# Mamba-2 scan and SiLU block on one core: unit 0's second y bank copied by VectorE, and the first 385 entries in a new order

## The chip, the core and the metric

The kernel runs on one NeuronCore of a Trainium2 chip. Five engines with a queue each work side by side: TensorE (PE, with its weight loads as PEld), VectorE (DVE), ScalarE (ACT), GpSimd (POOL) and SyncE (SP), which here only issues DMAs. Instructions of one engine run in the order in which they were written; a semaphore wait at the head of a queue holds everything behind it. Matmuls write PSUM, which is read by VectorE and ScalarE. The metric is the device time of the whole program in microseconds (us). The kernel before has a median of 329.49 us over 3 runs (328.6 to 329.88).

## What is computed

A chunked state-space scan over 4 batches, 8 heads and 768 positions (head size 32, state size 16), then a feed-forward block with SiLU over the 3072 resulting rows of 256:

```python
log_a = np.log(np.clip(a, 1e-06, 1.0))
for c in range(nc):                       # chunks of the sequence
    cum = np.cumsum(la, axis=-1)
    L = np.exp(cum[:, :, :, None] - cum[:, :, None, :]) * causal
    M = np.einsum('bhin,bhjn->bhij', Cc, Bc) * L
    y_intra = np.einsum('bhij,bhjd->bhid', M, xc)
    y_inter = np.einsum('bhin,bhnd->bhid', Cc, state) * np.exp(cum)[:, :, :, None]
    y[:, :, sl] = y_intra + y_inter
    state = decay_full[:, :, None, None] * state + np.sum(Bx, axis=2)
# then, with x = y as 3072 rows of 256
h = x @ w_in                              # 256 x 2048
out = (h * (1.0 / (1.0 + np.exp(-h)))) @ w_out    # 2048 x 256
```

The two weight matrices come in as 8-byte numbers, so each tile of them is turned into 4-byte numbers on the chip.

## The kernel before

The 3072 positions are 12 units of 256 (three to a batch); two units make a pair, so there are six pairs. Each unit passes through the scan (a few small matmuls, and elementwise work on VectorE, ScalarE and GpSimd) and gives y; each pair then passes through w_in, SiLU and w_out. Pair 0 takes the feed-forward block in plain 4-byte matmuls (`f_s1`, `f_n`); the later pairs take it in split operands of a faster matmul type.

Nothing schedules the kernel when it is built. The text `SCHEDULE` lists 1309 entries; each is a short name with numbers, and the last loop of the kernel calls the function of each entry in turn (`DO`). So the place of an entry in the text is the place of its instructions in the queue of their engine, and of its DMA in the queue that issues it (`QUEUES`: 0 is SP, 1 is ACT, 2 is POOL). `SLOTS` says which buffer of a pool each new tile takes, by an explicit list: `s2k` and `r4k` are SBUF slots, `raw` the slots for incoming weights, `hp` three PSUM banks that rotate under most matmul results.

The entries that matter here, for unit u (lines of the kernel before in brackets):

- Loads. `Lt,u,1,g` is a quarter of C in the layout that VectorE transposes, four of them for a unit (L262); `Ln` is half of B or C (L254), `Lx` half of x (L269), `ia` and `ip` parts of a (L375, L379), `lw,n` one weight tile of 512 KB: 0 to 7 of w_in, 8 to 15 of w_out (L288). All of these are on SP, except two `Ln` of unit 0 on ACT.
- `z` is one matmul of zeros that keeps TensorE busy and whose result is not used (L441); there are 36 of them, all in the opening.
- Decays. `A` clips a (L448); `AT` transposes it on TensorE (L453) and `AU` copies it out (L457); `as` spreads it (L495 on VectorE, L497 on ScalarE); `ab` transposes that (L502); `E` is a scan on VectorE that makes the decay matrix of one half unit (L512). `P01` makes the running products (L475, L479).
- Scan of unit 0 and 1. `T` transposes C on VectorE and needs all four `Lt` (L525); `ce` scales it on ScalarE (L546); `tp` and `tq` transpose B and copy it out (L531, L540); `B` and `C` are products on GpSimd or VectorE (L520, L551); `D` is the state matmul, which needs both halves of x and of `B` (L571); `g0` is C times B (L585); `M` multiplies it by the decays on VectorE, two halves (L600); `S` advances the state, four steps (L613, L615); `SM` masks it on ScalarE, two halves (L623); `Y` is the matmul that gives y in two PSUM banks, `ga` and `gb` (L635, L644).
- `X0,u,w` copies one y bank out of PSUM on ScalarE (L666); the two copies of a unit fill its part of the tile that `s` reads.
- Pair 0 in w_in. `s,u,j` is the matmul of unit u with weight tile j (L697; four matmuls, 128x256 each, two records each in the trace); `si` is its SiLU on ScalarE (L703). `n1` is a matmul with a tile of w_out (L761). `a`, `d` and `q` are the matmuls of later pairs (L800, L782).
- Weights. `u` and `v` take the two words of a weight tile apart on ScalarE (L294, L297); `w,n,0`, `w,n,1`, `w,n,2` work on them on VectorE (L303, L307, L310); `W` adds them on GpSimd (L318). `H`, `lD`, `dD`, `Wl`, `Wd` make the split operands (L322 to L335).

Of the kernel before, what the change touches and what calls it, by code (L numbers as in the profile page):

```python
# [888 lines left out]
```

## Time and profile before

| | us |
|---|---|
| median of 3 runs | 329.49 |
| profiled execution, whole time | 329.1 |
| its span, first to last instruction | 327.4 |
| TensorE busy | 320.3 |
| VectorE busy | 240.4 |
| ScalarE busy | 209.5 |
| GpSimd busy | 56.0 |

The span is 1.7 us shorter than the execution's own time. Times in the rows of the trace count from the start of the span. In a timeline row the first number is the start, the second how long the row lasts, then the engine (with a q where it is the queue that issues a DMA), the line, the operation, what it writes and reads, the shapes, and how many instructions are merged; in square brackets stands how long the engine was idle just before and what ended that. In a row of windows stand the stretch, its length, then for each engine the busy time and the number of instructions, the granted clock, the share of the DMA engines in use and GB/s.

### The profile page before, as it was taken

To read this page: it belongs to the slowest core of one execution; us is meant where nothing else is said; L and a number is where in the kernel's file an instruction comes from. 1 tells how busy PE (TensorE), PEld (TensorE's weight loads), DVE (VectorE), ACT (ScalarE), POOL (GpSimd) and SP (SyncE) were. 2 spreads that over 40 slices of the span, in tenths; PEclk is the share of its full clock that TensorE was granted. 3 is DMA by queue.
4 is the path that set the end of the run, shared out by engine and by line. 5 is a ranking of instruction groups with operands and counts; after the bars stand their busy time and mean duration, and the time that the engine had idled before them with its cause. 6 is when DMAs were issued, how large, how long until landed. Compare 5 with 4: busy or idle time off the path is not lost.

```text
span 327.4 us, 7519 instructions
## 1 busy us (share of the span) xinstructions
PE 320.3 (98%) x3064; PEld 243.4 (74%) x3067; DVE 240.4 (73%) x331; ACT 209.5 (64%) x319; POOL 56.0 (17%) x74
## 2 busy tenths in 40 slices
PE   8999999999999999999999999999999999999994
PEld 3478576655687777878887778878887788888883
...
DMA packets 94962, 29.27 MB, mean 89 GB/s; under 512 B 80000, under 2 KB 86912, under 8 KB 94928
## 3 DMA queue, kind: packets, MB, share of 16 engines
...
q14 instruction: 10, 0.08, 0.1%
...
## 4 chain that ended last, share of the span: by engine, by line
PE 94%; SPq 2%; DMA 1%; DVE 1%; issue 1%; DVEq 0%
PE hp L782 29%; PE ga L800 18%; PE gb L800 18%; PE hp L761 9%; PE hp L697 6%; PE o_ps L782 6%; PE ga L635 2%; PE ga L585 2%; PE ga L644 2%; DMA s2k<-in_C_dram 1%; PE gb L644 1%; PE ga L571 1%; SPq L262 0%; SPq L375 0%; PE o_ps L531 0%
## 5 line engine op out<-in xcount | busy, mean ns | idle before, releaser
L782 PE MATMUL hp<-r4k,s2k 128*128 128x512 f32 x400 | 110.0, 394 | 0.0
L651 DVE SCALAR_TENSOR_TENSOR r4k<-r4k,r4k 128x1024 fp32r<-128x1024 f32 (+1 forms) x42 | 50.5, 1202 | 51.3 <-ACT r4k L827 48.2
L782 PEld LDWEIGHTS hp<-r4k,s2k 128*128 128x128 f32 x400 | 74.0, 188 | 16.4 <-issue 0.3
L800 PE MATMUL ga<-raw,s2k 128*128 128x512 f32 x240 | 62.3, 395 | 0.0
L800 PE MATMUL gb<-raw,s2k 128*128 128x512 f32 x240 | 61.1, 390 | 0.0
L800 PEld LDWEIGHTS ga<-raw,s2k 128*128 128x128 f32 x240 | 44.7, 188 | 11.4 <-ACT ga L811 0.9
L800 PEld LDWEIGHTS gb<-raw,s2k 128*128 128x128 f32 x240 | 44.8, 188 | 9.9 <-ACT gb L811 0.5
L837 DVE SCALAR_TENSOR_TENSOR r4k<-r4k,r4k 128x1024 fp32r<-128x1024 f32 x40 | 49.2, 1231 | 3.4 <-DVE r4k L651 0.9
L827 ACT ACTIVATE r4k<-r4k 128x1024 fp32r<-128x1024 f32 x40 | 42.2, 1058 | 3.2 <-issue 1.3
L811 ACT ACTIVATE ga<-ga 128x1024 f32<-128x1024 f32 x21 | 21.1, 1007 | 24.6 <-PE ga L800 23.8
L811 ACT ACTIVATE gb<-gb 128x1024 f32<-128x1024 f32 x21 | 21.2, 1009 | 17.6 <-PE gb L800 13.3
L782 PE MATMUL o_ps<-r4k,s2k 128*128 128x512 f32 x80 | 30.7, 390 | 0.0
L761 PE MATMUL hp<-r4k,s2k 128*128 128x512 f32 x64 | 30.0, 602 | 0.0
L821 ACT ACTIVATE r4k<-gb 128x1024 f32<-128x1024 f32 x21 | 21.4, 1021 | 12.4 <-PE gb L800 9.9
L520 POOL TENSOR_TENSOR BT<-bn,ab 128x256 f32<-128x256 f32 x10 | 6.7, 672 | 129.5 <-DVE ab L512 123.3
L318 POOL TENSOR_TENSOR s2k<-s2k,s2k 128x512 uint32<-128x512 uint32 (+1 forms) x19 | 23.6, 1250 | 26.4 <-DVE s2k L307 13.7
L821 ACT ACTIVATE r4k<-ga 128x1024 f32<-128x1024 f32 x21 | 21.5, 1023 | 8.4 <-PE ga L800 8.2
L512 DVE TENSOR_TENSOR_SCAN ab<-ab,diag 128x512 f32<-128x512 f32 x20 | 24.8, 1265 | 0.0
L697 PE MATMUL hp<-r4k,s2k 128*128 128x256 f32 x96 | 22.3, 382 | 0.2 <-issue 0.2
L697 PEld LDWEIGHTS hp<-r4k,s2k 128*128 128x128 f32 x96 | 18.0, 190 | 4.0 <-issue 1.4
L761 PEld LDWEIGHTS hp<-r4k,s2k 128*128 128x128 f32 x64 | 11.6, 189 | 10.5 <-issue 9.6
L782 PEld LDWEIGHTS o_ps<-r4k,s2k 128*128 128x128 f32 x80 | 15.0, 188 | 3.2
...
## 6 DMA issues: line engine op xcount, KB each, us to landing
...
raw<-in_moe_w_in_dram SPq DMA_DIRECT2D x8, 512.0 KB, 4.2
raw<-in_moe_w_out_dram SPq DMA_DIRECT2D x8, 512.0 KB, 8.0
...
```

Of the source, the lines that this page charges most:

```text
L318: nc.gpsimd.tensor_tensor(out=u[:, :, fs], in0=u[:, :, fs], in1=v[:, :, fs], op=ALU.add)
L512: nc.vector.tensor_tensor_scan(out=o, data0=src, data1=diag.rearrange("p h t -> p (h t)"), initial=0.0, op0=ALU.mult, op1=ALU.add)
L644: nc.tensor.matmul(out=y[w][32 * q:32 * q + 32, c, 64 * k:64 * k + 64], lhsT=xc[64 * c:64 * c + 64, k, h], rhs=m[64 * c:64 * c + 64, k, h] ...
L651: nc.vector.scalar_tensor_tensor(out=l, in0=f32(h), scalar=BACK, in1=y, op0=ALU.mult, op1=ALU.add)
L697: nc.tensor.matmul(out=hp[:, i], lhsT=WT[j][:, kc, 128 * i:128 * i + 128], rhs=XM()[:, 2 * kc:2 * kc + 2, u], start=(kc == 0), stop=(kc == ...
L761: nc.tensor.matmul(out=NP[m], lhsT=WT[8 + f // 2][:, f % 2, 128 * m:128 * m + 128], rhs=GT[0, f // 2][:, f % 2], start=(n == 1), stop=(n = ...
L782: nc.tensor.matmul(out=ACC[P, c], lhsT=WK[8 + i, p][:, k, 128 * m:128 * m + 128], rhs={"h": HT, "l": LT, "d": DT}[p][P, i][:, k], start=(n ...
L800: nc.tensor.matmul(out=o, lhsT=WK[j, q][:, kc, 128 * i:128 * i + 128], rhs=xs[:, 2 * kc:2 * kc + 2], start=(start and q == "h" and kc == 0 ...
L811: nc.scalar.activation(t, t, AF.Copy, scale=1.0 + Z)
L821: nc.scalar.activation(g, t, AF.Silu, scale=BACK)
L827: nc.scalar.activation(t, GT[G, i], AF.Copy, scale=-LESS * Z)
L837: nc.vector.scalar_tensor_tensor(out=DT[G, i], in0=f32(HT[G, i]), scalar=-1.0, in1=f32(LT[G, i]), op0=ALU.mult, op1=ALU.subtract)
```

## The change

One function is new, and one entry uses it: unit 0's bank 1 of y, before the entry `X0,0,1` on ScalarE, is now copied by `Xd,0,1` on VectorE. The other bank stays on ScalarE (`X0,0,0`). The first 385 entries stand in a new order, the other 924 entries are as before. Apart from the one replaced entry the two lists hold the same entries; `H,0` moves from entry 224 to entry 385. The lists of slots change with the order. Two more new functions (a weight copy by DMA and a spill to DRAM) are added to the table and used by no entry.

```diff
 SCHEDULE = """
-Ln,0,0,0,1 ia,1 ci z,1 z,1 z,1 z,1 z,1 z,1 ia,0 Ln,0,0,1,1 cI z,1 ch cP ct ip,0,0 z,1 z,1 z,1 c1 cd A AT cp AU lw,0 z,1
-z,1 as,0,0 ab,0,0 P01,0,0 P01,0,1 as,0,1 ab,0,1 as,1,1 ab,1,1 E,0,0 u,0 z,1 z,1 z,1 Lt,0,1,3,0 v,0 w,0,0 w,0,2 w,0,1
-lw,4 W,0,1 z,1 B,0,0 z,1 z,1 v,4 Lt,0,1,1,0 u,4 z,1 z,1 Ln,1,1,1,0 z,1 E,0,1 B,0,1 z,1 z,1 z,1 Lt,0,1,0,0 Lt,0,1,2,0
-T,0,1 as,1,0 z,1 z,1 z,1 tp,0 tq,0 E,1,1 Lx,0,0,0 Lx,0,1,0 D,0 S,0,0 z,1 w,4,2 z,1 S,0,1 z,1 w,4,0 S,0,2 ce,0,0 ce,0,1
-g0,0 M,0,1 lw,7 v,7 Ln,1,0,0,0 SM,0,0 M,0,0 z,1 z,1 SM,0,1 u,7 w,4,1 w,7,0 z,1 z,1 w,7,2 w,7,1 lw,5 v,5 w,5,2 W,0,0
-S,0,3 Ln,1,1,0,0 ab,1,0 E,1,0 C,0 Y,0 X0,0,1 Ln,1,0,1,0 B,1,1 X0,0,0 u,5 w,5,0 ip,1,0 z,1 P01,1,0 tp,1 tq,1 s,0,0 ce,1,1
-ce,1,0 g0,1 Lx,1,1,0 Lx,1,0,0 W,4 xh,0 w,5,1 si,0,0 B,1,0 P01,1,1 D,1 s,0,4 M,1,1 lw,1 u,1 lw,12 S,1,0 W,5 v,1 ca S,1,1
-S,1,2 SM,1,0 SM,1,1 lw,13 s,0,5 si,0,5 v,12 C,1 M,1,0 Y,1 w,1,0 w,1,1 W,7 si,0,4 lw,8 w,1,2 W,1,0 z,1 w,12,2 X0,1,0 H,7
-S,1,3 X0,1,1 x,0,0 lD,7 u,12 w,12,0 w,12,1 u,13 w,13,0 w,13,1 W,1,1 s,0,1 u,8 v,8 s,1,5 ir,3 w,8,0 si,0,1 s,1,0 co
...
+Lt,0,1,1,0 ca ci z,1 z,1 z,1 z,1 z,1 z,1 z,1 c1 z,1 z,1 z,1 z,1 cp z,1 z,1 z,1 z,1 cd z,1 z,1 z,1 Ln,0,0,0,1 cI ia,0 ch
+cP co z,1 Ln,0,0,1,1 ip,0,0 P01,0,0 P01,0,1 ct Lt,0,1,3,0 ia,1 A lw,0 AT AU as,0,0 Ln,1,1,1,0 z,1 z,1 u,0 w,0,0 w,0,1
+lw,4 ab,0,0 tp,0 Lt,0,1,0,0 as,0,1 ab,0,1 as,1,1 ab,1,1 v,0 tq,0 E,0,0 B,0,0 z,1 z,1 Lt,0,1,2,0 z,1 z,1 T,0,1 ce,0,0 C,0
+z,1 E,0,1 B,0,1 E,1,1 Lx,0,1,0 w,0,2 v,4 ce,0,1 Lx,0,0,0 z,1 W,0,0 z,1 as,1,0 u,4 z,1 z,1 z,1 lw,7 D,0 S,0,0 g0,0
+Ln,1,0,1,0 w,4,0 B,1,1 M,0,0 z,1 S,0,1 S,0,2 v,7 SM,0,0 M,0,1 w,4,2 SM,0,1 w,4,1 W,0,1 z,1 ab,1,0 lw,5 W,4 E,1,0 v,5 z,1
+u,5 Ln,1,1,0,0 z,1 Y,0 Xd,0,1 X0,0,0 w,7,2 S,0,3 w,5,0 w,5,1 Ln,1,0,0,0 B,1,0 z,1 u,7 lw,1 tp,1 tq,1 ce,1,1 ip,1,0
+P01,1,0 ce,1,0 w,5,2 W,5 Lx,1,0,0 s,0,0 P01,1,1 v,1 Lx,1,1,0 g0,1 D,1 M,1,0 lw,13 si,0,0 S,1,0 S,1,1 lw,12 xh,0 u,1
+w,1,0 C,1 S,1,2 w,1,1 SM,1,1 u,13 w,1,2 W,1,0 s,0,4 SM,1,0 s,0,5 M,1,1 S,1,3 w,7,0 w,13,0 u,12 x,0,0 lw,8 v,12 Y,1
+X0,1,0 w,7,1 W,1,1 s,0,1 X0,1,1 si,0,4 w,12,2 xh,1 x,1,0 si,0,5 W,7 w,12,0 w,12,1 v,8 u,8 H,7 w,8,0 w,8,1 Ln,2,0,1,0
...
+    def f_XD(u, w):
+        y, c0 = YO[u]
+        nc.vector.tensor_copy(out=XM()[:, 2 * w:2 * w + 2, u], in_=y[w][:, :, c0:c0 + 128])
...
-        "Y": f_Y, "X0": f_X0, "y": f_YS, "xh": f_XH, "x": f_XL, "lw": load_w, "u": lambda n: w_size(n, "u"),
+        "Y": f_Y, "X0": f_X0, "Xd": f_XD, "y": f_YS, "xh": f_XH, "x": f_XL, "lw": load_w, "u": lambda n: w_size(n, "u"),
```

More of the change, by code (lines that the diff above doesn't have):

```diff
@@ L335, in w_part, with w_copy @@
         nc.scalar.activation(t, f32(WK[n, "h"]), AF.Copy, scale=1.0 if p == "l" else Z)
+    def w_copy(n):
+        t = WK[n, "l"] = small(f"l{n}", [128, 2, WF], FR)
+        nc.sync.dma_start(out=f32(t).rearrange("p k f -> p (k f)"), in_=f32(WK[n, "h"]).rearrange("p k f -> p (k f)"))
     def w_more(n, p):
```

43 lines of the change are left out of this document (25 added, 18 removed), and 6 rows, old and new, of the table SLOTS.

## The prediction

> **What bounds the kernel.** I read the page first, then busy time by stretch, then the chain of waits through the opening, then the timelines of the engines there.
>
> ```profile
> span 327.4 us, 7519 instructions
> PE 94%; SPq 2%; DMA 1%; DVE 1%; issue 1%; DVEq 0%
> 0.00:17.94 17.94, 15.60 (x208) 8.25 (x210) 13.23 (x35) 9.67 (x20) 4.54 (x16) 1.00 0.80 178
> 17.94:26.41 8.47, 8.19 (x187) 6.55 (x186) 7.30 (x17) 6.01 (x13) 6.22 (x8) 1.00 0.86 255
> 26.41:320.00 293.59, 293.59 (x2659) 226.62 (x2659) 217.15 (x274) 192.68 (x286) 45.21 (x52) 1.00 0.41 80
> ```
>
> 94% of the chain that ended last is TensorE. In a row of windows the third number is TensorE's busy time: from 26.41 us to 320 us it never rests (293.59 of 293.59). So the end is the time at which that dense stretch begins, plus a fixed amount. It begins with `s,0,1` at 26.41 us. All that TensorE runs ahead of `s,0,1` is the same in both orders: the same 36 `z`, the same 16 other entries. The change can move the end only by idle time of TensorE ahead of that point, or by a new stall behind it. Visible idle ahead of it is 17.94-15.60=2.34 us and 8.47-8.19=0.28 us, 2.62 us in all.
>
> ```profile
> 6.36 4.75 DMA s2k<-in_C_dram
> 11.30 0.65 DVE ct L525
> 14.38 1.21 DVE ab L600 x2
> 17.25 0.27 PE o_ps L531
> ```
>
> This is the chain inside the opening: the last of the four `Lt` loads lands at 6.36+4.75=11.11 us, `T` transposes it at 11.30, VectorE reaches the two `M` at 14.38, `Y,0` and `tp,1` follow, then `s,0,0`. So in the opening the order of VectorE behind `T` sets the pace.
>
> ```profile
> 1.27 4.45 PE L441 MATMUL o_ps<-s2k 128*128 128x512 bf16 x10 [1.27 <-DVE s2k L388]
> 5.65 0.31 PE L453 MATMUL o_ps<-ident,s2k 32*128 32x32 f32 x1
> 6.70 1.53 PE L502 MATMUL hp<-ident,s2k 128*128 128x128 f32 x12
> 8.07 3.40 PE L441 MATMUL o_ps<-s2k 128*128 128x512 bf16 x15
> 15.73 0.27 PE L635 MATMUL ga<-cw,sm 32*64 32x64 f32 x2 [0.42 <-DVE ab L600]
> 17.94 1.99 PE L697 MATMUL hp<-r4k,s2k 128*128 128x256 f32 x8
> 20.68 0.46 PE L571 MATMUL hp<-s2k,BT 64*32 64x64 f32 x32
> 24.77 0.27 PE L635 MATMUL ga<-cw,sm 32*64 32x64 f32 x2
> 26.41 7.07 PE L697 MATMUL hp<-r4k,s2k 128*128 128x256 f32 x32 [0.16 <-issue]
> ```
>
> The places to follow: `AT` 5.65, `ab` 6.70, `Y,0` 15.73, `s,0,0` 17.94, `D,1` 20.68, `Y,1` 24.77, `s,0,1` 26.41. From `s,0,0` to `Y,1` TensorE takes 6.83 us; from `Y,1` to `s,0,1` 1.64 us, of which one `z`. A `z` costs 3.40/15, some 0.22 us.
>
> **1. More `z` ahead of `AT`.** 19 instead of 10. Nine at 0.22 are 2.0 us, so `AT` goes from 5.65 to about 7.6 (the first ten are slow, 4.45/10; if a further one is, 7.9). The second part of a, now fifth on SP instead of first, is there by then: in the order before `AT` had it at 5.65 at the latest, and four issues of about 0.5 to 0.7 us go ahead of it. From `AT` to `ab` takes 1.05 us, so `ab,0,0` starts at 8.65 and `E,0,0` can start at about 9.3 and ends at about 10.4. Before, it ran at 7.50. This costs the path nothing as long as `T` waits for its load longer than that; if the load is early, 10.4 is the floor for `T`.
>
> **2. VectorE behind `T`.** The largest term.
>
> ```profile
> 9.87 1.22 DVE L512 TENSOR_TENSOR_SCAN ab<-hp,diag 128x512 f32<-128x512 f32 x1
> 11.30 0.65 DVE L525 STREAM_TRANSPOSE ct<-s2k 128x256 f32<-128x256 f32 x1 [0.21 <-DMA s2k<-in_C_dram]
> 11.79 1.17 DVE L512 TENSOR_TENSOR_SCAN ab<-hp,diag 128x512 f32<-128x512 f32 x1
> 12.87 0.20 DVE L613 COPY st<-hp 128x64 f32<-128x64 f32 x1
> 12.98 0.68 DVE L310 SCALAR_TENSOR_TENSOR s2k<-raw,s2k 128x512 uint32<-128x512 uint32 x1
> 13.58 0.28 DVE L615 SCALAR_TENSOR_TENSOR st<-st,s2k,hp 128x64 f32<-128x64 f32 x1
> 13.77 0.42 DVE L303 TENSOR_SCALAR s2k<-s2k 128x512 f32<-128x512 f32 x1
> 14.11 0.28 DVE L615 SCALAR_TENSOR_TENSOR st<-st,s2k,hp 128x64 f32<-128x64 f32 x1
> 14.30 0.69 DVE L600 TENSOR_TENSOR ab<-gb,ab 128x512 f32<-128x512 f32 x1
> 14.90 0.69 DVE L600 TENSOR_TENSOR ab<-ga,ab 128x512 f32<-128x512 f32 x1
> ```
>
> Before, `E,0,1` (9.87) runs while `T`'s load is still coming, so only `E,1,1` is left behind `T`. From start to start: `T` 0.49, a scan 1.08, the copy `S,0,0` 0.11, `w,n,2` 0.60, `S` 0.19, `w,n,0` or `w,n,1` 0.34, `M` 0.60. The second `M` starts 3.60 us after `T`. In the new order `T` stands ahead of `E,0,1`, and then come `E,0,1 E,1,1 w,0,2 S,0,0 w,4,0 M,0,0 S,0,1 S,0,2 M,0,1`: 0.49+1.08+1.08+0.60+0.11+0.34+0.60+0.19+0.19=4.68 us. One scan has gone from the cover of a DMA onto the path: +1.08.
>
> When does `T` start? The last two `Lt` are 9th and 10th on SP in both orders, with the same ten loads up to them, so I keep 11.30. Lower end 10.4 (step 1), as two small loads now run in the idle start; upper end 11.6, as the first weight tile is issued two places later. With 11.30, `M,0,1` starts at 15.98 and `Y,0`, 0.83 later as before (14.90 to 15.73), at 16.81: +1.08.
>
> **3. The y copy.**
>
> ```profile
> 17.25 0.37 ACT L666 ACTIVATE r4k<-gb 128x256 f32<-128x256 f32 x1
> 17.51 0.38 ACT L666 ACTIVATE r4k<-ga 128x256 f32<-128x256 f32 x1
> 323.62 0.42 DVE L747 COPY s2k<-gb 128x256 f32<-128x256 f32 x1 [0.42 <-PE gb L739]
> ```
>
> ScalarE needs 0.64 us for both banks (17.25 to 17.89). VectorE's nearest row is the same shape from the same PSUM tile: 0.42 us. But `Xd` stands behind `w,4,2`, `w,4,1` and `E,1,0`: it starts 0.60+0.60+0.34+1.08=2.62 us after `M,0,1`, at 18.60, and ends at 19.02. ScalarE's copy starts 1.52 us after `Y,0` (15.73 to 17.25), at 18.33, and ends at 18.70; its own second copy would have ended at 18.97. So `Xd` brings nothing here, 0.0, and puts about 0.34 us on VectorE (ends: -0.27 if VectorE were free at once, +0.3 if TensorE waited for all of it). `s,0,0` reads bank 0 first and bank 1 from its third record on, 0.43 us later, so it starts at 18.75 without a further wait: +0.81 (`tp,1`, which before came last at 17.25 to 17.94, is no longer last).
>
> **4. To `Y,1`.** TensorE alone: 18.75+6.83=25.58. VectorE, from `Xd`: `Xd` 0.34, `w,7,2` 0.60, `S,0,3` 0.19, `w,5,0` and `w,5,1` 0.68, `P01` 0.42 and 0.61, `w,5,2` 0.60, `M,1,0` 0.60, two `S` 0.38, `w,1,0` 0.34, `C,1` 0.34, `S` 0.19, `w,1,1` 0.34, `w,1,2` 0.60 are 6.23 us, so `M,1,1` starts at 24.83 and frees `Y,1` 0.83 later, at 25.66. The two meet within 0.1 us. From there to `s,0,1` it is 1.64-0.22=1.42, since the `z` behind `Y,1` has moved to the front: 27.08. Against 26.41 that is +0.67.
>
> **5. Two loads that are now waited for.**
>
> ```profile
> 18.12 1.03 SPq L288 DMA_DIRECT2D raw<-in_moe_w_in_dram  x1
> 19.19 1.50 SPq L288 DMA_DIRECT2D raw<-in_moe_w_out_dram  x3
> 22.10 0.69 ACT L294 ACTIVATE s2k<-raw 128x512 f32<-128x512 f32 x1 [1.52 <-DMA raw<-in_moe_w_in_dram]
> 23.26 0.68 ACT L623 ACTIVATE sm<-st,par 128x128 f32<-128x128 f32 x2
> 25.41 0.70 ACT L297 ACTIVATE s2k<-raw 128x512 f32<-128x512 uint32 x1
> raw<-in_moe_w_in_dram SPq DMA_DIRECT2D x8, 512.0 KB, 4.2
> raw<-in_moe_w_out_dram SPq DMA_DIRECT2D x8, 512.0 KB, 8.0
> 16.00:18.00 2.00, 1.83 (x92) 1.39 (x82) 1.86 (x4) 1.44 (x5) 0.34 (x1) 1.00 0.70 118
> 20.00:22.00 2.00, 1.88 (x68) 1.50 (x67) 2.00 (x5) 0.57 (x1) 1.43 (x2) 1.00 0.91 280
> ```
>
> `lw,1` now goes ahead of unit 1's x on SP. `D,1` needs that x, at 18.75+2.74=21.49; before it was there by 20.68. At 280 GB/s 512 KB are 1.9 us, so x is there by 22.6 at worst; but the DMA engines were at 0.70 from 16 to 18 us, where `lw,1` fills 0.6 us, and 21.4 is as near. The wait of `D,1` lies between 0 and 1.1.
>
> On ScalarE `u,13` now stands between `SM,1,1` and `SM,1,0`, and `Y,1` is behind `SM,1,0`. So `Y,1` waits for `lw,13`, the first w_out tile, 22nd on SP as `lw,12` was before (issued at 19.19). A w_in tile took 4.0 us from issue (18.12) to the wait's end (22.10); `lw,12` was read at 25.41, 6.2 us after its issue, and the page's median for w_out is 8.0. Landing lies between 23.2 and 27.2. Behind it come `u,13` 0.58, `SM` 0.34 and the start of `Y,1`, 1.1 us in all: `Y,1` at 24.3, 26.5 or 28.3 against 25.66, a cost of 0, 0.8 or 2.6. I take 0.25 for the two loads together, nearer to no wait, since the idle DMA time ahead of it is now used.
>
> The Trainium skill (DMA: Bandwidth & Descriptors, Anatomy of one DMA — SWDGE (gpsimd) path) fits a transfer as 2.0 us plus its bytes over 436 GB/s, for loads that GpSimd issues; by it `lw,13` would take an estimated 3.2 us, `Y,1` would not wait, and the sum would be +0.67. The trace's 4.0 and 6.2 us for SP's loads do not agree with it.
>
> **6. The rest.** `SM,0,0` and `SM,0,1` stay behind `v,7` as before. The `H,0` that moves later has no reader until `lD,0`, after the entry where it now stands. Behind `s,0,1` VectorE holds about the same work as before, and TensorE comes 0.7 us later, which is more slack; I cost this at nothing. The cover is that VectorE is 217.15 of 293.59 us busy there; the next thing late would be `W,13` for `n1,11,0`.
>
> **Sum.** `M` behind one more scan +1.08, `tp,1`'s wait gone -0.27, so `s,0,0` +0.81; the `z` already spent -0.22; VectorE meeting TensorE at `Y,1` +0.08; loads +0.25: +0.92, or +0.9. The profiled execution took 329.1, with 327.4 of span; it would be 330.0. The median is 0.4 above that execution, so 330.4.
>
> **Rivals.**
> (a) The forecast, +0.3 to +1.4 around 330.4. Chance 0.52.
> (b) Slower by over 0.5% (1.65 us, about what a measurement of this kernel can tell from no change). One mechanism: `SM,1,0` behind `u,13` behind `lw,13`. It decides from a landing at 25.5 us on: `Y,1` then starts at 26.6 and `s,0,1` at 28.06. With the 8.0 us of the page it lands at 27.2 and the time is 329.5+3.3=332.8. For it: `lw,12` in the same place was read only at 25.41. Against it: DMA engines that stood partly idle just before. Chance 0.30, a stall behind `s,0,1` that I do not see included.
> (c) `T`'s load lands early and `T` starts at the floor, 10.4. Then all of steps 2 to 4 is 0.9 earlier: `Y,1` at 24.76, `s,0,1` at 26.18, -0.2, time 329.3. For it: two of the four `Lt` leave earlier. Against it: the last two do not. Chance 0.18. Only a part of it is faster by over 0.5%: of the 2.62 us of idle 1.27 is the start, which stays, and the other 1.35 is less than 1.65.
>
> **How the numbers follow.** Time of (a), 330.4; its own range 329.8 to 330.9. The range for 8 in 10 runs from (c), 329.2, to within (b), 332.3. Faster 0.06 (the tail of (c), idle that the rows hide), same 0.64, slower 0.30.
>
> **What would show it.** `AT` near 7.6; `T` near 11.3 with an idle VectorE before it and `E,0,1` behind it; the second `M` 4.7 us after `T`; `Xd` starting after ScalarE's copy; `s,0,0` near 18.75; TensorE idle before `D,1` or `Y,1`, with `SM,1,0` directly behind a `u` that waited for a DMA. The prediction is wrong if `T` starts by 10.5, if `Y,1` starts after 26.6, or if TensorE rests behind `s,0,1`.

## The result, and the profile after

The changed kernel takes 331.21 us (median of 4 runs, 331.07 to 331.36), the kernel before 329.08 us on the same chip (4 runs). The ratio is 1.006, 95% interval 1.0041 to 1.0079: slower by 0.4 to 0.8%, some 2.1 us. The profiled execution took 331.11 us with a span of 329.4 us, 2.0 more than before. The prediction's 330.4 us was 0.8 us short. The time is inside the prediction's range (329.2 to 332.3) and above the forecast's own range, which ended at 330.9. As a difference the forecast missed by more: it had +0.9 over a kernel before of 329.49, and +2.1 was measured over 329.08. The prediction drew its line between "same" and "slower" at 0.5%; the interval reaches from just below that line to above it.

First the page's chain and the busy time by stretch (the third number is TensorE's):

```profile
PE 87%; DVE 4%; POOL 3%; SPq 2%; ACT 1%; DMA 1%; issue 1%; DVEq 0%
19.16:28.14 8.98, 8.38 (x186) 6.19 (x184) 8.84 (x21) 6.17 (x14) 3.80 (x5) 1.00 0.91 238
28.14:322.00 293.86, 293.78 (x2665) 226.49 (x2660) 213.60 (x273) 192.09 (x285) 48.78 (x50) 1.00 0.40 78
```

TensorE's share of the chain has gone from 94 to 87%, and VectorE and GpSimd have come in. In the first stretch, from `s,0,0` to `s,0,1`, VectorE is busy for 8.84 of 8.98 us: it has become the engine that sets the pace there. In the second TensorE still never seems to rest, though it loses another half microsecond there; that has to be looked for step by step. TensorE's timeline, rows that answer to those before the change:

```profile
7.81 0.24 PE L457 MATMUL o_ps<-ident,s2k 32*128 32x32 f32 x1
17.20 0.27 PE L639 MATMUL ga<-cw,sm 32*64 32x64 f32 x2 [1.08 <-ACT sm L627]
19.16 1.91 PE L705 MATMUL hp<-r4k,s2k 128*128 128x256 f32 x8
21.62 0.72 PE L575 MATMUL hp<-s2k,BT 64*32 64x64 f32 x32
22.27 1.99 PE L705 MATMUL hp<-r4k,s2k 128*128 128x256 f32 x8
24.84 1.97 PE L705 MATMUL hp<-r4k,s2k 128*128 128x256 f32 x8 [0.57 <-DVE st L619]
26.73 0.27 PE L639 MATMUL ga<-cw,sm 32*64 32x64 f32 x2
28.14 7.17 PE L705 MATMUL hp<-r4k,s2k 128*128 128x256 f32 x32
44.72 1.89 PE L705 MATMUL hp<-r4k,s2k 128*128 128x256 f32 x8
49.98 1.99 PE L705 MATMUL hp<-r4k,s2k 128*128 128x256 f32 x8
```

These are `AT`, `Y,0`, `s,0,0`, `D,1`, `s,0,4`, `s,0,5`, `Y,1`, `s,0,1` (one row with the entries behind it), `s,1,1` and `s,1,2` (behind the change the lines are 4 to 18 higher than before). The last two answer to these rows of the kernel before:

```profile
42.88 1.89 PE L697 MATMUL hp<-r4k,s2k 128*128 128x256 f32 x8
47.75 1.89 PE L697 MATMUL hp<-r4k,s2k 128*128 128x256 f32 x8
```

| start, us | before | predicted | after | after less before |
|---|---|---|---|---|
| `T` | 11.30 | 11.30 | 11.55 | +0.25 |
| `Y,0` | 15.73 | 16.81 | 17.20 | +1.47 |
| `s,0,0` | 17.94 | 18.75 | 19.16 | +1.22 |
| `D,1` | 20.68 | 21.49 | 21.62 | +0.94 |
| `Y,1` | 24.77 | 25.91 | 26.73 | +1.96 |
| `s,0,1` | 26.41 | 27.33 | 28.14 | +1.73 |
| `s,1,1` | 42.88 | as `s,0,1` | 44.72 | +1.84 |
| `s,1,2` | 47.75 | as `s,0,1` | 49.98 | +2.23 |

(In the column of the prediction the 0.25 us that it took for the loads stand ahead of `Y,1`.) Three places carry the loss: the way to `s,0,0`, +1.22; the way from `D,1` to `Y,1`, where the lag doubles; and the step from `s,1,1` to `s,1,2`, 5.26 us instead of 4.87. Behind that the lag of TensorE's rows moves little: 2.33 us near 60 us, some 2.2 us from about 118 to 250 us, and 2.0 us from about 295 us to the end. Between `s,0,1` and `s,1,1` another 0.11 us arises, whose cause no run isolates.

VectorE behind `T`, in its timeline:

```profile
11.55 0.64 DVE L529 STREAM_TRANSPOSE ct<-s2k 128x256 f32<-128x256 f32 x1 [0.79 <-DMA s2k<-in_x_dram]
12.04 2.27 DVE L516 TENSOR_TENSOR_SCAN ab<-hp,diag 128x512 f32<-128x512 f32 x2
16.38 0.68 DVE L604 TENSOR_TENSOR ab<-gb,ab 128x512 f32<-128x512 f32 x1
19.05 0.40 DVE L674 COPY r4k<-gb 128x256 f32<-128x256 f32 x1
24.42 0.27 DVE L619 SCALAR_TENSOR_TENSOR st<-st,s2k,hp 128x64 f32<-128x64 f32 x1
25.55 0.68 DVE L604 TENSOR_TENSOR ab<-gb,ab 128x512 f32<-128x512 f32 x1
```

It rests 0.79 us ahead of `T`, and both scans stand behind `T`; the second `M` (16.38) starts 4.83 us after `T`. `Xd` (19.05) starts 0.59 us after ScalarE's copy (18.46) and lasts 0.40. `S,1,2` (24.42) is the last reader of the PSUM buffer that holds `D,1`'s first result, and `s,0,5` writes that same buffer (slot 2 of `hp`): TensorE rests for it until 24.84.

The profile names a load of x for `T`'s rest, but `T` reads only C. By the DMA records the last load of C landed at 11.35 us, against 11.11 in the kernel before, and `T` starts 0.2 us after it in both. So `T`'s +0.25 us is that load.

One run below, the one with the scan and a weight step moved together, was profiled at a granted clock of 0.852; only its times are used.

### The profile page after: what moved, and what is told of

Its sections match the earlier page's. It is cut to its first block, busy times and chain, and to the rows that moved or that the text cites. A ratio compares the mean times of both kernels' runs of the same rounds, so it can differ in the third digit from the quotient of the medians.

```text
span 329.4 us, 7517 instructions
## 1 busy us (share of the span) xinstructions
PE 321.3 (98%) x3067; PEld 243.3 (74%) x3067; DVE 238.1 (72%) x332; ACT 209.1 (63%) x318; POOL 59.3 (18%) x74
## 4 chain that ended last, share of the span: by engine, by line
PE 87%; DVE 4%; POOL 3%; SPq 2%; ACT 1%; DMA 1%; issue 1%; DVEq 0%
PE hp L800 28%; PE ga L818 17%; PE gb L818 17%; PE hp L779 6%; PE o_ps L800 6%; PE hp L705 5%; POOL s2k L318 2%; PE ga L639 2%; PE ga L648 2%; PE ga L589 2%; DMA s2k<-in_x_dram 1%; PE gb L648 1%; PE ga L575 1%; DVE s2k L310 1%; DVE ab L516 1%
## 5 line engine op out<-in xcount | busy, mean ns | idle before, releaser
L800 PEld LDWEIGHTS hp<-r4k,s2k 128*128 128x128 f32 x400 | 74.0, 188 | 16.3 <-issue 0.3
L318 POOL TENSOR_TENSOR s2k<-s2k,s2k 128x512 uint32<-128x512 uint32 (+1 forms) x19 | 27.5, 1451 | 23.5 <-DVE s2k L310 14.6
L705 PEld LDWEIGHTS hp<-r4k,s2k 128*128 128x128 f32 x96 | 17.7, 190 | 5.3 <-issue 1.7
```

Source lines behind the costliest of these rows:

```text
L318: nc.gpsimd.tensor_tensor(out=u[:, :, fs], in0=u[:, :, fs], in1=v[:, :, fs], op=ALU.add)
L705: nc.tensor.matmul(out=hp[:, i], lhsT=WT[j][:, kc, 128 * i:128 * i + 128], rhs=XM()[:, 2 * kc:2 * kc + 2, u], start=(kc == 0), stop=(kc == ...
L800: nc.tensor.matmul(out=ACC[P, c], lhsT=WK[8 + i, p][:, k, 128 * m:128 * m + 128], rhs={"h": HT, "l": LT, "d": DT}[p][P, i][:, k], start=(n ...
```

## Experiments

The two theories at the start. **Mine**: VectorE is the limit from `T` to `Y,1`; each of its instructions that was put ahead of that, the copy among them, is paid, and the rest is the wait of `s,0,5`. **The rival**: the late loads (unit 1's x behind `lw,1`, `lw,13` ahead of `SM,1,0`) set the time and VectorE merely fills. For the part behind `s,0,1` there was a third question. In the diffs only the entries that move are shown; each tile keeps its slot. Beside these runs the kernel before took 329.5 us (35 runs at the end, 329.52 median), and distances "above the kernel before" count from there. The changed kernel itself was not run again beside them; its 331.21 us stand 1.7 above the 329.52 and 2.1 above the 329.08 of its own measurement, so a comparison of a version with it carries some 0.4 us of doubt.

### The copy back on ScalarE

```diff
-Y,0 Xd,0,1 X0,0,0
+Y,0 X0,0,0 X0,0,1
```

> The changed kernel with the y copy given back to ScalarE (X0,0,0 then X0,0,1), the new order kept. Theory: the copy on VectorE brings nothing, because s,0,0 starts at 19.16 us right behind TensorE's transposes (18.72 us, four of them) and needs the second bank only from its third matmul on. s,0,0 stays at 19.1 to 19.2 us; VectorE gets its 0.32 us back, so S,1,2 (24.42 us) and with it s,0,5 (24.84 us) and Y,1 (26.73 us) come up to 0.3 us earlier; time 1.8 us above the kernel before (the changed kernel: 2.1). Rival: the copy saves ScalarE's second copy (0.29 us from start to start in the trace of before), so s,0,0 starts 0.3 us later and the time is 2.4 us above the kernel before.

Measured: 331.02 us, ratio 1.0042 (1.0023 to 1.0061), 1.5 us above the kernel before. TensorE's `s,0,0`, `s,0,5` and `Y,1`:

```profile
19.06 1.89 PE L705 MATMUL hp<-r4k,s2k 128*128 128x256 f32 x8
24.41 1.97 PE L705 MATMUL hp<-r4k,s2k 128*128 128x256 f32 x8 [0.46 <-DVE st L619]
26.30 0.27 PE L639 MATMUL ga<-cw,sm 32*64 32x64 f32 x2
```

`s,0,0` is not later without `Xd` (19.06 against 19.16), and everything that hangs on VectorE behind it is 0.43 us earlier, which is the copy's own 0.40. In the new order the copy on VectorE is a loss of about 0.4 us in these steps. Theory held, with a larger gain in the steps than the 0.3 us expected. In the times it doesn't show clearly: the median is only 0.2 us below the changed kernel's.

### The copy in the old order

Besides the copy, four entries of VectorE move behind it (`w,7,1`, `w,5,2`, `S,0,3`, `E,1,0`), so that VectorE can take it in time.

```diff
-w,7,2 w,7,1 lw,5 v,5 w,5,2 W,0,0 S,0,3 Ln,1,1,0,0 ab,1,0 E,1,0 C,0 Y,0 X0,0,1
+w,7,2 lw,5 v,5 W,0,0 Ln,1,1,0,0 ab,1,0 C,0 Y,0 Xd,0,1 w,7,1 w,5,2 S,0,3 E,1,0
```

> The kernel before with one part of the change alone: the y copy X0,0,1 given to VectorE, and taken as early there as VectorE can (w,7,1, w,5,2, S,0,3 and E,1,0 behind it); the order of all other entries is the old one. Theory (from the run with the copy given back to ScalarE): it is not the copy that costs or saves much. Y,0 ends near 17.1 us, the copy can run from 17.2 to 17.6 us beside ScalarE's, s,0,0 starts at 17.6 to 17.7 us instead of 17.94; VectorE's work behind it is 0.4 us later, so Y,1 gains nothing or loses up to 0.3 us. Time within 0.3 us of the kernel before, on either side. Rival: the copy is worth what ScalarE saves, 0.3 us from s,0,0 to the end: time 0.3 us or more below the kernel before, every later step of TensorE 0.3 us earlier.

Measured: 329.49 us, ratio 1.0002 (0.998 to 1.0023). TensorE's `s,0,0`, `D,1`, `s,0,5`, `s,0,1`:

```profile
17.76 1.89 PE L701 MATMUL hp<-r4k,s2k 128*128 128x256 f32 x8
20.68 0.55 PE L571 MATMUL hp<-s2k,BT 64*32 64x64 f32 x32 [0.40 <-POOL BT L520]
23.34 1.97 PE L701 MATMUL hp<-r4k,s2k 128*128 128x256 f32 x8 [0.18 <-DVE st L615]
26.87 2.32 PE L701 MATMUL hp<-r4k,s2k 128*128 128x256 f32 x10 [0.16 <-issue]
```

`s,0,0` gains 0.18 us (17.76, a little less than the 17.6 to 17.7 expected), `D,1` is where it was, and `s,0,5` waits for the same state step as in the changed kernel. In this execution `s,0,1` is 0.46 us late; in the times there is no difference that can be told from none. The copy by itself is not what made the kernel slower by 2 us.

### The same, with VectorE's work behind it rearranged

```diff
-Xd,0,1 w,7,1 w,5,2 S,0,3 E,1,0 ... s,0,4 M,1,1 lw,1 ... S,1,2 SM,1,0
+Xd,0,1 E,1,0 S,0,3 w,7,1 w,5,2 ... s,0,4 lw,1 ... S,1,2 M,1,1 SM,1,0
```

> The kernel of the run with the y copy alone in the old order, with what that run showed as its cost taken away: behind the copy VectorE takes E,1,0 and S,0,3 ahead of w,7,1 and w,5,2 (there E,1,0 came 0.4 us later, D,1's B with it, and s,0,5 waited for S,1,2), and M,1,1 stands behind S,1,2. Theory: s,0,0 at 17.7 to 17.8 us (before 17.94), s,0,5 at 22.6 to 22.9 (before 22.90), s,0,1 at 26.1 to 26.4 (before 26.41); time 0.0 to 0.3 us below the kernel before, which the timing can hardly tell from none, but the steps of TensorE can. Rival: VectorE has no room for the copy between Y,0 and Y,1 in any order: s,0,1 at 26.7 us or later, time 0.2 to 0.6 us above.

Measured: 330.27 us, ratio 1.0011 (0.9989 to 1.0032): not told from the kernel before, and not faster; its median is 0.75 us above the 329.52. `s,0,0`, `D,1`, `s,0,1`:

```profile
17.52 1.89 PE L701 MATMUL hp<-r4k,s2k 128*128 128x256 f32 x8
20.72 0.46 PE L571 MATMUL hp<-s2k,BT 64*32 64x64 f32 x32 [0.69 <-DMA s2k<-in_x_dram]
26.51 2.70 PE L701 MATMUL hp<-r4k,s2k 128*128 128x256 f32 x10 [0.27 <-POOL s2k L318]
```

Here `s,0,0` is 0.42 us earlier than before, and all of it ends at `D,1`, which waits 0.69 us for x. The x that the kernel before finds ready at 20.68 is ready only just then: by the DMA records it landed at 20.54 us there and at 20.59 in this run. A saving ahead of it is worth nothing as long as that load stands where it does. Neither the theory (0.0 to 0.3 us faster) nor the rival (VectorE has no room) had that.

### The scan behind `T` alone, in the old order

```diff
-E,0,1 B,0,1 z,1 z,1 z,1 Lt,0,1,0,0 Lt,0,1,2,0 T,0,1 as,1,0
+z,1 z,1 z,1 Lt,0,1,0,0 Lt,0,1,2,0 T,0,1 E,0,1 B,0,1 as,1,0
```

> The kernel before with one part of the new order alone: E,0,1 and, on GpSimd, B,0,1 directly behind T,0,1. Theory: T waits for its load until 11.28 us in either order, so it stays at 11.30, VectorE rests 1.2 to 1.3 us ahead of it instead of 0.21, and all of VectorE's work behind it is 1.0 to 1.1 us later: the state steps, the gates SM and Y,0 (15.73 us before) at 16.7 to 16.9, s,0,0 (17.94) at 18.9 to 19.1. Up to Y,1 VectorE keeps that lag, s,0,1 (26.41) at 27.2 to 27.6. Time 0.8 to 1.5 us above the kernel before: half of the change's cost or more. Rival: VectorE has room behind T and takes most of it back by s,0,0: s,0,0 at 18.3 or earlier, time within 0.4 us of the kernel before.

Measured: 330.17 us, ratio 1.0024 (1.0004 to 1.0044): 0.65 us above the kernel before. The profiled execution took 331.46, 1.3 above the median, so its later steps do not stand for the median. What it does show, on VectorE (`T` and `w,4,2`):

```profile
11.22 0.65 DVE L525 STREAM_TRANSPOSE ct<-s2k 128x256 f32<-128x256 f32 x1 [0.93 <-DMA s2k<-in_C_dram]
14.03 1.21 DVE L310 SCALAR_TENSOR_TENSOR s2k<-raw,s2k 128x512 uint32<-128x512 uint32 x1
```

`T` stays and VectorE rests 0.93 us ahead of it. The second `M` starts 5.26 us after `T`, against 3.60 in the kernel before: 1.08 of that is the scan, and `w,4,2` lasts 1.21 us here instead of 0.68. By the medians the move alone costs 0.65 us, less than the 1.08 of the scan and between the two forecasts (0.8 to 1.5 by the theory, at most 0.4 by the rival): about a third of what the change costs.

### The scan put ahead of `T` again, in the new order

```diff
-T,0,1 ce,0,0 C,0 z,1 E,0,1 B,0,1
+E,0,1 T,0,1 ce,0,0 C,0 z,1 B,0,1
```

> The changed kernel with unit 0's second scan E,0,1 back ahead of T,0,1 on VectorE. Theory: VectorE is the limit up to Y,0 and again up to S,1,2. In the changed kernel it rests 0.79 us ahead of T (11.55 us), and the scan of 1.08 us stands behind it: filling the rest brings Y,0 from 17.20 to about 16.4 us, s,0,0 from 19.16 to about 18.4. D,1 still waits for its x until 22.0 us (landed at 21.96), but S,1,2 now ends by 24.0, when s,0,4 frees TensorE, so the rest of 0.57 us ahead of s,0,5 goes: s,0,5 at 24.0 to 24.1, Y,1 at 26.0 (SM,1,0 is done at 25.99), s,0,1 at 27.4 instead of 28.14. Time 1.0 to 1.5 us above the kernel before. Rival: the two late loads (x for D,1, the weight ahead of SM,1,0) set the time; s,0,5 and Y,1 move by no more than 0.2 us, time 2.0 to 2.2 us above.

Measured: 331.69 us, ratio 1.0061 (1.0041 to 1.0081): nothing gained. VectorE's timeline:

```profile
9.50 2.33 DVE L516 TENSOR_TENSOR_SCAN ab<-hp,diag 128x512 f32<-128x512 f32 x2
11.75 0.62 DVE L529 STREAM_TRANSPOSE ct<-s2k 128x256 f32<-128x256 f32 x1
13.97 0.21 DVE L617 COPY st<-hp 128x64 f32<-128x64 f32 x1
14.99 0.52 DVE L303 TENSOR_SCALAR s2k<-s2k 128x512 f32<-128x512 f32 x1 [0.82 <-ACT s2k L294]
15.43 0.68 DVE L604 TENSOR_TENSOR ab<-ga,ab 128x512 f32<-128x512 f32 x1
```

The rest ahead of `T` is filled, and by `S,0,0` (13.97, changed kernel 14.81) VectorE is 0.84 us ahead. Then it gives all of it back: `w,4,0` waits 0.82 us for `u,4` on ScalarE, and `M,0,0` behind it starts at 15.43 instead of 15.28. ScalarE's queue from `T` on is `ce,0,0 v,4 ce,0,1 as,1,0 u,4`, so `u,4` hangs on `T` as VectorE does, and `T` is 0.2 us later here. In the new order two chains of the same length lead from `T` to `M`. My theory was wrong in taking VectorE's order alone for the limit. `T` is late because the scan ahead of it cannot start before 9.50: `AT`, on which it hangs, is 2.2 us later in the new order.

The rival is not excluded by this run. In its profiled execution (332.21 us, 0.5 above the median) unit 1's x landed at 22.31 and 22.90 us by the DMA records, 0.95 us later than in the changed kernel, `D,1` waited 0.76 us for it, and `s,0,1` came at 29.07.

### The scan and `w,4,0` moved together

```diff
-T,0,1 ce,0,0 C,0 z,1 E,0,1 B,0,1 ... Ln,1,0,1,0 w,4,0 B,1,1 M,0,0 z,1 S,0,1 S,0,2 v,7 SM,0,0 M,0,1
+E,0,1 T,0,1 ce,0,0 C,0 z,1 B,0,1 ... Ln,1,0,1,0 B,1,1 M,0,0 z,1 S,0,1 S,0,2 v,7 SM,0,0 M,0,1 w,4,0
```

> The changed kernel with the scan E,0,1 ahead of T,0,1, as in the run before, and besides w,4,0 behind M,0,1 on VectorE. The run with the scan alone showed VectorE 0.8 us earlier up to 14.2 us and then resting 0.82 us ahead of w,4,0 (14.99 us) for ScalarE's u,4, which stands behind both ce copies and so hangs on T (11.75 us). Theory: two chains of equal length lead from T to M,0,0, one through the scans on VectorE, one through ScalarE to w,4,0; only with both cut does Y,0 come earlier. M,0,0 then starts at 14.2 to 14.4 us instead of 15.28, the gates SM at 15.5, Y,0 at 16.1 to 16.3 us instead of 17.20, s,0,0 at 18.1 to 18.3. D,1 waits for x until about 22 us, s,0,4 at 22.2 to 22.5, s,0,5 without a rest at 24.0 to 24.3, Y,1 at 26.0 to 26.2, s,0,1 at 27.3 to 27.6. Time 1.3 to 1.8 us above the kernel before. Rival: Y,0 hangs on something else than these two (the loads or TensorE): Y,0 stays at 17.0 to 17.3 us and the time at 2.0 us or more above.

Measured: 331.23 us, ratio 1.005 (1.0029 to 1.0072), 1.6 us above the kernel before and within what was expected; against the changed kernel's 331.21 nothing is gained. The steps are read from the next run, whose order is the same up to the end of `Y,0`: there `M,0,0` starts at 14.91 and `Y,0` at 16.84, where 14.2 to 14.4 and 16.1 to 16.3 were expected.

### Everything ahead of `s,0,1` at once

To the moves of the last run (the expectation has the state steps directly behind `D,1`; in the edit `M,1,0` still stands ahead of them, as the diff shows):

```diff
-Y,0 Xd,0,1 X0,0,0 ... lw,1 tp,1 ... s,0,0 P01,1,1 v,1 Lx,1,1,0 g0,1 D,1 M,1,0 lw,13 si,0,0 S,1,0 S,1,1 lw,12 xh,0 u,1
-w,1,0 C,1 S,1,2 w,1,1 SM,1,1 u,13 w,1,2 W,1,0 s,0,4 SM,1,0 s,0,5 M,1,1 S,1,3 w,7,0
+Y,0 X0,0,0 X0,0,1 ... tp,1 ... s,0,0 P01,1,1 Lx,1,1,0 lw,1 g0,1 D,1 M,1,0 lw,13 si,0,0 S,1,0 S,1,1 S,1,2 lw,12 xh,0 C,1
+SM,1,1 s,0,4 SM,1,0 s,0,5 M,1,1 v,1 u,1 w,1,0 w,1,1 w,1,2 W,1,0 S,1,3 u,13 w,7,0
```

> The kernel of the run with the scan and w,4,0 moved, and besides: the y copy back on ScalarE, unit 1's x loaded ahead of lw,1 as in the kernel before, the state steps S,1,0 to S,1,2 directly behind D,1, SM,1,0 ahead of u,13, and v,1, u,1, w,1,0 to w,1,2 behind M,1,1. Theory: these are all of the places that cost the changed kernel time up to s,0,1. Y,0 at 16.1 to 16.4 us, s,0,0 at 18.0 to 18.3, x for D,1 landed by 21.2 us, s,0,4 at 21.1 to 21.6, s,0,5 at 22.9 to 23.5, Y,1 at 24.8 to 25.4, s,0,1 at 26.3 to 27.0 (before 26.41, changed 28.14). Time 0 to 0.9 us above the kernel before, the rest being what arises behind s,0,1. Rival: the new order's other moves ahead of s,0,1 cost as well (more work on VectorE ahead of Y,1): s,0,1 at 27.4 us or later, time 1.3 us or more above.

Measured: 332.79 us, ratio 1.0091 (1.0061 to 1.0122): the slowest but for the run with VectorE at rest further down, and on the rival's side. VectorE's `T` and `M,0,0`, then TensorE's `Y,0` and `s,0,1`, then its longest wait:

```profile
11.90 0.64 DVE L529 STREAM_TRANSPOSE ct<-s2k 128x256 f32<-128x256 f32 x1
14.91 0.69 DVE L604 TENSOR_TENSOR ab<-ga,ab 128x512 f32<-128x512 f32 x1 [0.56 <-issue]
16.84 0.27 PE L639 MATMUL ga<-cw,sm 32*64 32x64 f32 x2 [0.64 <-ACT sm L627]
28.32 2.00 PE L705 MATMUL hp<-r4k,s2k 128*128 128x256 f32 x8 [1.02 <-POOL s2k L318]
PE hp L779 <- POOL s2k L318: 1.7, 1, 1.7
```

With both chains cut `M,0,0` starts 3.01 us after `T` instead of 3.73, and ahead of it VectorE rests 0.56 us. The profile names no releaser for that rest. `M,0,0` reads TensorE's `g0,0`, whose last record starts at 14.52, and `g0,0` could start at 14.09 for two reasons that lie within 0.05 us of each other. `ce,0,1` on ScalarE, which stands behind `T`, ended at 14.04. And `D,0` on TensorE waited until 13.73 for GpSimd's `B,0,1`, which stands behind `C,0` and so behind `T` too. So at least a third chain leads from `T` to `M`, and a fourth is as close. About 0.7 us are to be had there and not the 1.1 I expected. `Y,1` comes at 25.82, 0.9 us earlier than in the changed kernel. Then my own edit costs more than it saved: `w,1,0` to `w,1,2` behind `M,1,1` make `W,1,0` late, `s,0,1` waits 1.02 us for it, and near 40 us an `n1` waits 1.7 us for another sum on GpSimd. I had looked at `Y,1` and not at what `s,0,1` needs besides.

### The state steps ahead of `M,1,0`

```diff
-D,1 M,1,0 lw,13 si,0,0 S,1,0 S,1,1 lw,12 xh,0 u,1 w,1,0 C,1 S,1,2
+D,1 lw,13 si,0,0 S,1,0 S,1,1 S,1,2 M,1,0 lw,12 xh,0 u,1 w,1,0 C,1
```

> The changed kernel with unit 1's three state steps S,1,0 to S,1,2 taken ahead of M,1,0, w,1,0 and C,1 on VectorE, nothing else moved. Theory: s,0,5 writes the PSUM buffer from which S,1,2 still reads D,1's first result; in the changed kernel S,1,2 runs at 24.42 us, behind 0.67, 0.42 and 0.42 us of other VectorE work, and s,0,5 rests 0.57 us for it. Here S,1,2 ends by 23.3 us, s,0,5 starts at 24.0 to 24.1 us without a rest, and Y,1 then hangs on M,1,1 and SM,1,0: 26.2 to 26.4 us instead of 26.73. Time 1.6 to 1.8 us above the kernel before. Rival: the rest ahead of s,0,5 follows from D,1's late x alone (its wait to 22.0 us): s,0,5 stays at 24.8, time 2.0 to 2.2 us above.

Measured: 331.81 us, ratio 1.0077 (1.0048 to 1.0106): 2.3 above the kernel before where 1.6 to 1.8 was expected, no gain. TensorE's `s,0,4` and `s,0,5`, now one row, and two of its waits:

```profile
22.13 3.76 PE L705 MATMUL hp<-r4k,s2k 128*128 128x256 f32 x16
PE gb L639 <- DVE ab L604: 0.5, 1, 0.5
PE hp L779 <- POOL s2k L318: 1.0, 1, 1.0
```

The two run back to back (`s,0,5` at 23.96), with `D,1` as late as in the changed kernel (21.63): the rest in the changed kernel was the shared PSUM buffer and the place of `S,1,2`, not the load. But `Y,1`'s second half now waits 0.5 us for `M,1,1`, so `s,0,1` gains 0.1 us (28.04). VectorE is full there, and moving one of its steps forward moves the wait to another. The 1.0 us for a GpSimd sum is new.

### The SiLU behind the weights

```diff
-si,1,0 v,13 w,13,2 u,6 w,6,0 ir,1 ir,0 v,6 w,6,2
+v,13 w,13,2 u,6 w,6,0 ir,1 ir,0 v,6 si,1,0 w,6,2
```

> The changed kernel with one ScalarE instruction moved: si,1,0 (35.35 us, which waits for TensorE's result with a rest of 2.86 us ahead of it) behind v,13, u,6 and v,6, which wait for nothing that late. All up to s,0,1 (28.14 us) stays, 1.73 us behind the kernel before. Theory: the further 0.6 us that arise between 28 and 48 us come from that order: v,14 late, w,14,2 late (39.66 us), the sum W,6 late on GpSimd and beside VectorE (5.25 us long), H,6 and lD,6 late, AD and W,2 late, s,1,2 at 49.98 us. With si,1,0 behind the weights w,14,2 starts about 0.9 us earlier, TensorE's lag at s,1,2 falls from 2.23 to about 1.7 us and the time is 1.4 to 1.6 us above the kernel before. Rival: the 0.6 us are TensorE's own lag working through and not this order: the lag at s,1,2 stays at 2.2 us and the time 2.0 to 2.2 us above.

Measured: 331.35 us, ratio 1.0053 (1.0033 to 1.0072), 1.8 us above; the theory's 1.4 to 1.6 was missed. VectorE's `w,14,2`, then the sum `W,6` on GpSimd:

```profile
38.88 0.92 DVE L310 SCALAR_TENSOR_TENSOR s2k<-raw,s2k 128x512 uint32<-128x512 uint32 x1 [0.83 <-ACT s2k L297]
41.63 5.26 POOL L318 TENSOR_TENSOR s2k<-s2k,s2k 128x512 uint32<-128x512 uint32 x1 [0.70 <-DVE s2k L307]
```

`w,14,2` came 0.78 us earlier as meant, `W,6` did not, and it was as slow. ScalarE's order was not the cause of its length.

### The sum `W,6` beside a resting VectorE

```diff
-W,6 n1,11,1 AP AD,1 H,12 Wl,12 v,2 Ln,2,0,0,0 H,6 H,1 ... Lt,3,1,3,0 lD,6 dD,6
+W,6 H,6 lD,6 n1,11,1 AP AD,1 H,12 Wl,12 v,2 Ln,2,0,0,0 H,1 ... Lt,3,1,3,0 dD,6
```

> The changed kernel with H,6 and lD,6 directly behind the sum W,6, so that VectorE, which runs its entries in order, rests while GpSimd takes that sum. In the changed kernel W,6 took 5.25 us (41.49 to 46.74), VectorE being busy without a gap from 41.34 to 45.6 us; other sums of the same size took 1.28 to 1.40 us beside a resting VectorE. Theory: a sum on GpSimd and VectorE's work on the same memory shut each other out. W,6 then takes 1.2 to 1.5 us. Rival: the sum is slow for another reason (what it reads arrives late, or its record is off): it still takes 4 us or more. The time is not what this run is for, VectorE's later work being 2 to 3 us behind: 1 to 4 us above the kernel before.

First the changed kernel: `W,6` on GpSimd, and the first and last of the seven VectorE instructions that follow one another without a rest from 41.34 to 45.6 us, then the two halves of `W,2`, the next sum on GpSimd, ahead of `s,1,2`.

```profile
41.49 5.25 POOL L318 TENSOR_TENSOR s2k<-s2k,s2k 128x512 uint32<-128x512 uint32 x1 [1.30 <-DVE s2k L307]
41.34 1.22 DVE L490 TENSOR_TENSOR_SCAN r4k<-r4k,r4k 48x520 f32<-48x520 f32 x1
44.95 0.67 DVE L310 SCALAR_TENSOR_TENSOR s2k<-raw,s2k 128x512 uint32<-128x512 uint32 x1
47.94 1.99 POOL L318 TENSOR_TENSOR s2k<-s2k,s2k 128x256 uint32<-128x256 uint32 x2
```

And the run with VectorE at rest:

```profile
41.56 1.27 POOL L318 TENSOR_TENSOR s2k<-s2k,s2k 128x512 uint32<-128x512 uint32 x1 [1.30 <-DVE s2k L307]
48.51 5.12 POOL L318 TENSOR_TENSOR s2k<-s2k,s2k 128x256 uint32<-128x256 uint32 x2 [1.06 <-DVE s2k L310]
```

1.27 us instead of 5.25, the same instruction started within 0.1 us of the same time; and in the second row the two halves of `W,2`, which in the changed kernel took 1.99 us, now fall beside a busy VectorE and take 5.12. The execution, a single one, took 336.64 us: VectorE's work is 3 us later, and TensorE rests 3.82 us ahead of `s,1,2` for `W,2`. That `W,6` makes no headway beside those seven instructions of VectorE, and does as soon as they are away, is shown.

It does not hold for every full VectorE. In the changed kernel `W,4` runs while VectorE is busy without a rest from 17.92 to 19.45 us:

```profile
18.08 1.27 POOL L318 TENSOR_TENSOR s2k<-s2k,s2k 128x512 uint32<-128x512 uint32 x1 [1.08 <-DVE s2k L307]
17.92 1.22 DVE L516 TENSOR_TENSOR_SCAN ab<-hp,diag 128x512 f32<-128x512 f32 x1
```

`W,4` takes its 1.27 us. The scan and `Xd` behind it each read one operand from PSUM (`hp`, `gb`). Beside `W,2` in the changed kernel VectorE gave way instead: an instruction of line 330 took 1.11 us instead of 0.68, and one of line 303 took 0.95 instead of 0.41. What decides who waits there is not shown.

### The sum `W,6` on VectorE

```diff
+            if n == 6:
+                nc.vector.scalar_tensor_tensor(out=u[:, :, fs], in0=u[:, :, fs], scalar=0x7fffffff, in1=v[:, :, fs],
+                                               op0=ALU.bitwise_and, op1=ALU.bitwise_or)
+                return
             nc.gpsimd.tensor_tensor(out=u[:, :, fs], in0=u[:, :, fs], in1=v[:, :, fs], op=ALU.add)
```

> The changed kernel with the one sum W,6 taken off GpSimd: VectorE combines the two words at the same place of its order (with a bitwise operation in place of the integer sum, so the weights of expert 6 are not the reference's). Theory: of TensorE's lag behind the kernel before, the part that arises behind s,0,1 (from 1.73 us at s,0,1 to 2.23 at s,1,2) comes from W,6's 5.25 us on GpSimd, behind which H,6, lD,6 and the halves of W,2 stand. VectorE needs about 0.6 us for it, H,6 runs at about 42 us instead of 46.78, lD,6 by 45 instead of 47.44; TensorE's step from s,1,1 to s,1,2 falls from 5.26 us to 4.9 to 5.0 (before 4.87), the lag at s,1,2 to 1.8 to 1.9 us, the time to 1.5 to 1.8 us above the kernel before. Rival: that part of the lag has another source; s,1,1 to s,1,2 stays at 5.2 us or more and the time at 2.1.

Measured: 330.71 us, ratio 1.0025 (1.0003 to 1.0047), 1.2 us above the kernel before. `s,1,1` and `s,1,2`:

```profile
44.93 1.89 PE L709 MATMUL hp<-r4k,s2k 128*128 128x256 f32 x8
49.80 1.89 PE L709 MATMUL hp<-r4k,s2k 128*128 128x256 f32 x8
```

The step between them is 4.87 us, just that of the kernel before. So the 0.4 us that the changed kernel loses in this step come from `W,6` on GpSimd: there the theory held. `s,1,1` is itself 0.2 us later than in the changed kernel, and the lag at `s,1,2` is 2.05 us, where 1.8 to 1.9 was expected. The time is 1.2 us above the kernel before, where 1.5 to 1.8 was expected. That is 0.5 us below the changed kernel by the medians and 0.9 by the distances from the kernel before; the two intervals overlap, so it is the step that shows the cause and not the time. This is not a version to use, as it changes the weights; it shows the size.

How the sum sets `s,1,2` can be read from the changed kernel's rows. GpSimd takes its work in order: `W,6`, two issues of DMAs, the two halves of `W,2` (47.94), and `s,1,2` reads what `W,2` makes. `s,1,2` starts 8.49 us after `W,6`. In three more runs it is 8.49 to 8.51 us as well, with a step of 5.27 to 5.30 us (the copy back on ScalarE, the scan ahead of `T`, and the last run below). Where TensorE reaches the place later than that in any case, the step is 4.85 to 4.87 us though `W,6` is as slow (the state steps first, the SiLU behind the weights, and everything at once). So a slow `W,6` is a floor under the start of `s,1,2`, and costs only what TensorE is ahead of that floor.

### The state steps first, and `W,13` ahead of GpSimd's other work

```diff
-AA,0 AD,4 lw,14 lw,2 v,14 AA,1 n1,9,1 u,15 n1,1,1 W,13
+AA,0 W,13 AD,4 lw,14 lw,2 v,14 AA,1 n1,9,1 u,15 n1,1,1
```

(On top of the run with the state steps first.)

> The kernel of the run with the state steps first (s,0,5 without its rest, yet slower than the changed kernel), and besides the sum W,13 on GpSimd directly behind AA,0, ahead of AD,4 and AA,1. Theory: what took that run's gain is one wait of 1.0 us of TensorE for W,13 (39.75 us there, 1.68 long) at the n1 product near 40 us; GpSimd takes its entries in order, AA,0, AD,4 and AA,1 stand ahead of W,13, and they had run beside VectorE and longer (1.05 for 0.60 us). Here W,13 starts at 37.6 to 38.2 us, is done by 39.8, the wait goes, and s,1,1 comes at 44.6 to 45.0 us instead of 45.88; time 1.5 to 2.1 us above the kernel before. Rival: TensorE waits at the next entry of GpSimd instead (AD,4 or AA,1, then 1.3 us later): s,1,1 at 44.9 or earlier, but s,1,2 later than 50.2 us and the time 2.1 us or more above.

Measured: 331.17 us, ratio 1.0049 (1.0034 to 1.0064), 1.65 us above the kernel before, where the run without this move was at 2.3. GpSimd's `W,13` and `W,6`:

```profile
38.51 1.28 POOL L318 TENSOR_TENSOR s2k<-s2k,s2k 128x512 uint32<-128x512 uint32 x1
42.20 5.25 POOL L318 TENSOR_TENSOR s2k<-s2k,s2k 128x512 uint32<-128x512 uint32 x1 [0.70 <-DVE s2k L307]
```

`W,13` took its 1.28 us by 39.8 and TensorE's wait of 1.0 us is gone. `W,6` is as slow as ever. `s,1,1` came at 45.39, later than expected, since in this execution (331.81, 0.64 above the median) a weight landed late and ScalarE rested 2.96 us for it, until 28.20. Theory held in its mechanism and in the time; `s,1,1` was missed. Against the changed kernel's 331.21 nothing is gained.

None of these versions beats the kernel before, and none takes the whole loss of the changed kernel away. The parts of the loss are shown one by one; that they add up to 2.1 us is not.

## Why the prediction was right or wrong

The time lies in the range, but by one of its own signs the prediction was wrong: it named `Y,1` after 26.6 as such a sign, and `Y,1` started at 26.73. Two of its steps failed, 4 and 6.

**Step 1** (`AT` near 7.6, free) was right for this order: 7.81, and VectorE still rested 0.79 us ahead of `T`.

**Step 2** was right for the order as it is: the second `M` 4.83 us after `T` against 4.68, and `T` late by 0.25 us. Its reading, that a scan goes from the cover of a DMA onto the path for 1.08, holds only in part. Alone in the old order the move costs 0.65 us; taken back in the new order it brings nothing, since ScalarE's `u,4` ahead of `w,4,0` is as late. Before, that second chain was not there: `u,4` stood ahead of `T`.

**Step 3** was right in the new order: `Xd` starts behind ScalarE's copy, brings `s,0,0` nothing and costs VectorE 0.4 (0.34 predicted). `s,0,0` came at 19.16 instead of 18.75: 0.25 of that is `T`, the rest 0.15 in step 2. One reading in it was off: `s,0,0` stood straight behind `tp,1`, which starts at 18.72 and which step 3 had as no longer the last to be waited for; the 0.27 us that it took off for that came even so. In the old order the copy did bring `s,0,0` something, 0.18 and 0.42 us in the two runs with it, and both were lost by `D,1`.

**Step 4 failed.** "TensorE alone: 18.75+6.83=25.58" took over the 6.83 us of before as if the TensorE entries between `s,0,0` and `Y,1` waited for nothing. They took 7.57 us. 0.74 of it lies between `s,0,4` and `s,0,5`, 2.57 us from start to start for 1.83: the PSUM buffer that `S,1,2` had not yet read. Before, `S,1,2` was done in time and the dependence left no mark in the trace. It can be read from the code: `s` and `D` take the same three buffers. VectorE's own line was nearer (`M,1,1` 6.50 us after `Xd`, 6.23 predicted), and the run with the state steps first shows that it would have held `Y,1` almost as long: with the rest gone `s,0,1` moved by 0.1 us. So VectorE's fullness is the cause and the buffer is where it showed.

**Step 5** had the size right and not its place. `D,1`'s row lasts 0.72 us instead of 0.46, 0.26 for x; and `SM,1,0` was not held by `lw,13`: `u,13` ran at 25.03 without a wait. By the DMA records `lw,13` landed at 23.97 us, 5.5 us after its issue at 18.51 and between the bounds of 23.2 and 27.2. The Trainium skill's fit for loads issued by GpSimd (DMA: Bandwidth & Descriptors, Anatomy of one DMA — SWDGE (gpsimd) path) had given an estimated 3.2 us, and this load of SP does not agree with it either. But the 0.26 us at `D,1` is not on the path: VectorE did not rest from 19.05 to 27.6 us, and `s,0,5` waited beyond it for `S,1,2`. That the 0.25 fills a place in the sum is luck. Rival (b) named the right side and the wrong mechanism; its chance of 0.30 had "a stall behind `s,0,1` that I do not see included". Such a stall did come, but only some 0.5 us of the loss arises behind `s,0,1`; the larger part arises ahead of it.

**Step 6 failed.** "I cost this at nothing", with VectorE's free time as the cover. VectorE being 74% busy was the wrong thing to look at: what counted was whether it rested while GpSimd had a sum to take. It did not at `W,6`, which cost 0.4 us at `s,1,2` and by the run without it 0.5 to 0.9 us in the time. `W,13`, which step 6 named as next, stood in time in the changed kernel and became late in three of the runs.

Summed: of 1.73 us at `s,0,1` the prediction had 0.92. The missing 0.81 are 0.4 ahead of `s,0,0` and 0.4 at `s,0,5` and `Y,1`; of the further 0.5 at `s,1,2`, 0.39 is step 6 and 0.11 has no cause that a run isolates. Rival (c) did not come: `T` was late, not early.
